# An FNet layer with an MLP in split fp16: x summed into memory in blocks 2 to 5 instead of copied in block 0, and a hand-written order that now reaches over block 1's first step

## The chip, the cores and the metric

The kernel runs on one core of a Trainium2 chip. Its engines, as the profile names them, are TensorE (PE, with its weight loads PEld), VectorE (DVE), ScalarE (ACT), GpSimd (POOL) and SyncE (SP); each runs its instructions in their order, and waits where one needs what another engine or a DMA has not finished. A DMA is issued by an engine (here SP, POOL, and at the start ACT) and then runs by itself on sixteen DMA engines that all queues share. The metric is the device time of one execution in microseconds. The time before is 1279.42 us, the median of three runs from 1277.15 to 1281.52.

## The reference

What is computed, cut to its core (x is 2048 × 576, w1 576 × 4608, w2 4608 × 576, all fp32; w1 and w2 are drawn with a spread of 0.4):

```python
xn = _layernorm(x)                                   # no scale, no shift
a = einsum("bsd,ed->bse", xn, dft_hid_re)
b = einsum("bsd,ed->bse", xn, dft_hid_im)
y = einsum("ts,bse->bte", dft_seq_re, a) - einsum("ts,bse->bte", dft_seq_im, b)
h = maximum(einsum("bsd,df->bsf", xn, w1), 0)
return x + y + einsum("bsf,fd->bsd", h, w2)
```

Every fp32 operand is used as an fp16 high part and an fp16 low part, scaled by a power of two that comes from the operand's largest magnitude; a product is then three matmuls (high by high, high by low, low by high).

## The kernel before

**Tiles and stages.** The 2048 tokens are sixteen tiles of 128 in four groups (g = 0 to 3) of four. The MLP's 4608 hidden columns are nine blocks (b = 0 to 8) of 512. Blocks 1 to 8 are steps (b, g), numbered n = 4 to 35: a step forms the seven products of a Strassen-like scheme for each of two halves (`pair_products`: P1, P2, P6, P5, P7, P3, P4; L498), while the second matmul of the step before it (`products2`, L569) is put between them. What `products2` yields is summed in an SBUF buffer (`blocks2`, L582 and L584), and four buffers a step go by an accumulating DMA of 288 KB on POOL's queue into a DRAM tensor (`add2`, L591, the tiles `spill`). After block 8 the hidden-dimension transform, and then the sequence transform, follow from about 830 us to the end; there x is no longer read, since `spill` holds it already.

**Block 0** does the same in plain products: `piece` and `group` (L396) for the first matmul, 24 matmuls a quarter for the second (`plain2`, L618), ReLU and split (`relu_high`, `relu_low`, L411, L419), a scaled copy (`block2`), and an accumulating DMA (`add0`). In block 0 stands everything that happens once too: loads of x (L149), layernorm statistics (`stats`, L281), the high and low parts of normalised x (L321, L324, L329, L330), and the DMA transposes that make xT of them (`transposes`, L351, on SP; tile 0 alone is transposed on PE, L362). For block 1's scheme sums of xT's quarters are needed: `sums_x`, `high_x`, `low_x` and `transpose_sums` (L470, L473), staged in two buffers.

**What sets the order.** In block 0 the order of all instructions is written by hand, as a table of words, ORDER; each word is a call. The ones that the text uses: `mx` (largest magnitude of a part of w1, L648), `pa` to `pd` (the power of two from it, by PE; L242, L251, then DVE L254 to L259, which gives the scale `c_sw`), `th`, `tl` (PE transposes), `ch_`, `cl` (their copies out of PSUM), `hi`, `xn`, `lo` (high part, centred x, low part), `T` (DMA transposes of a tile), `p0`, `p` (the products of one tile), `P` (those of a group, 512 wide), `m`, `e`, `ad` (second product, its copy, its DMA), `ts`, `tu`, `tv`, `tw` (sums of x: sum, high part, low part, transposes), `lw`, `L1`, `L2` (loads of w2 of block 0, w1 and w2 of block 1), `n*` (block 1's w1), `f` (matmuls on an idle tile, L867, to keep PE busy), and `cx` (x copied from DRAM into `spill`, on SP). Words on different engines go on side by side; on one engine they run in the table's order.

After the table `end_hand()` leaves the order of blocks 1 to 8 to the framework's scheduler, which places instructions by estimated times. There the loads, maxima and splits of the next block's w1 and w2 are a list `todo` of pieces, and the loop over n takes pieces from it at fixed places of a step (`ready`, three a step, and `brief`, seven; in step 4, one more at each call). The transition at the end of block 8 is by hand again.

## Time and profile before

| | |
|---|---|
| median of three runs | 1279.42 us (1277.15 to 1281.52) |
| the profiled execution, time and span | 1281.23 us, span 1279.4 us |
| granted PE clock, mean of the span | 0.992 |
| ACT and POOL busy | 752.7 us (59%), 201.3 us (16%) |
| moved by DMA | 176.30 MB, 138 GB/s on average |
| block 0 | 0 to 118.12 us |

Rows of the profile show the start or the sum in us, the busy time, the engine, the line of the kernel, the operation with its tiles (out<-in), its shape and its count. In a timeline the bracket is the idle time of the engine ahead of the row and what ended it. SPq and PEq are an engine's sequencer. In the table by stretches each engine has its busy time and its count of instructions, then come the granted PE clock (1.00 is full), the mean share in which the 16 DMA engines were busy (rounded from overlapping records, so that it can read above 1) and the bytes they moved.

### The profile page before, as it was taken

How to read it: one execution, taken by the hardware profiler on the slowest of the kernel's cores; microseconds unless marked ns; L12 is line 12 of the kernel's file. 1: busy time of each engine (PE TensorE's matmuls, PEld its weight loads, DVE VectorE, ACT ScalarE, POOL GpSimd, SP SyncE). 2: the span in 40 equal slices, each digit the busy share in tenths (PEclk: the TensorE clock that was granted, in tenths of full speed). 3: DMA queues.
4: the chain of work that ended last, by engine and by line, in shares of the span. 5: the costliest groups of instructions: out<-in, count | busy, mean ns of one | idle time of the engine just before them, and what ended most of it. 6: DMA issues, size and time to landing. Idle time of an engine off the chain costs nothing. (4 is left out here: it accounts for less than half of the span.)

```text
span 1279.4 us, 26178 instructions
## 1 busy us (share of the span) xinstructions
PE 1224.3 (96%) x10403; PEld 996.8 (78%) x10403; DVE 1021.8 (80%) x1974; ACT 752.7 (59%) x1334; POOL 201.3 (16%) x260
## 2 busy tenths in 40 slices
PE   5989899999999999999999999889999999999998
PEld 4956778888888888888887888666777777777777
DVE  7856798888988888788888879769876757888785
ACT  6644767676676676766766757545544445543332
POOL 2353111121111111111111111100111110000000
PEclk9999999999999999999999999989999999999999
DMA  7999756677657566666576677511655541155440
GB/s 214 231 219 215 148 122 142 136 151 153 130 119 160 133 147 134 134 150 124 122 155 140 147 196 165 94 36 67 195 116 148 116 101 24 57 192 160 155 127 33
DMA packets 129387, 176.30 MB, mean 138 GB/s; under 512 B 49648, under 2 KB 90096, under 8 KB 129264
## 3 DMA queue, kind: packets, MB, share of 16 engines
q1 hardware_dynamic: 103344, 127.17, 33.7%
q0 software_dynamic: 25344, 47.20, 26.9%
q8 instruction: 81, 1.33, 0.4%
q14 instruction: 42, 0.34, 0.1%
q10 hardware_dynamic: 576, 0.26, 0.1%
HBM read 112.53 MB, written 56.62 MB: 132 GB/s over the span
## 5 line engine op out<-in xcount | busy, mean ns | idle before, releaser
L569 PE MATMUL p<-w2s,h 128*128 128x288 f16 x2688 | 368.1, 287 | 8.5 <-DVE h L520 2.8
L1349 PE MATMUL p<-R,cs 128*128 128x288 f16 x2688 | 332.6, 287 | 5.6 <-DVE accs L1359 3.3
L1349 PEld LDWEIGHTS <-cs 128*128 128x128 f16 x2688 | 263.2, 98 | 74.9 <-issue 4.5
L569 PEld LDWEIGHTS <-h 128*128 128x128 f16 x2688 | 263.2, 98 | 72.9 <-issue 6.5
L498 PEld LDWEIGHTS <-dbuf 128*128 128x128 f16 x1568 | 153.8, 98 | 31.1 <-issue 9.6
L498 PEld LDWEIGHTS <-wbuf 128*128 128x128 f16 x1568 | 153.4, 98 | 23.8 <-issue 3.0
L766 ACT ACTIVATE cs<-tb,sc_c 128x1024 f16<-128x1024 f32 x56 | 64.0, 1148 | 86.6 <-PE p L1349 53.0
L505 ACT ACTIVATE h<-accs 128x256 f16<-128x256 f32 x128 | 52.2, 412 | 105.3 <-DVE accs L528 82.8
L498 PE MATMUL bank<-xT,dbuf 128*128 128x256 f16 x896 | 112.2, 274 | 0.9 <-ACT s L526 0.9
L498 PE MATMUL bank<-xT,wbuf 128*128 128x256 f16 x896 | 110.7, 273 | 0.0
L591 POOL DMA_DIRECT2D spill<-dbuf x70 | 61.2, 879 | 256.5 <-DVE dbuf L584 215.0
L520 DVE TENSOR_TENSOR h<-s,h 128x1024 f16<-128x1024 f32 x64 | 78.0, 1219 | 28.7 <-ACT h L517 28.4
L498 PE MATMUL bank<-accs,dbuf 128*128 128x256 f16 x672 | 87.1, 273 | 7.1 <-ACT accs L524 5.1
L770 DVE SCALAR_TENSOR_TENSOR cs<-tb,sc_c,cs 128x1024 f16<-128x1024 f32 x56 | 71.6, 1281 | 27.3 <-ACT cs L766 26.9
L498 PE MATMUL bank<-accs,wbuf 128*128 128x256 f16 x672 | 86.4, 272 | 1.9 <-DVE accs L528 1.0
L517 ACT ACTIVATE h<-s 128x1024 f16<-128x1024 f32 x64 | 67.6, 1056 | 20.5 <-DVE s L512 20.1
L766 ACT ACTIVATE cs<-accs,sc_c 128x1024 f16<-128x1024 f32 x39 | 44.2, 1146 | 55.5 <-PE p L1349 25.6
L591 POOL DMA_DIRECT2D spill<-wbuf x42 | 37.1, 884 | 206.2 <-DVE wbuf L584 195.2
L1051 ACT ACTIVATE f<-f 128x1024 f32<-128x1024 f32 x64 | 67.0, 1046 | 0.0
L506 DVE SCALAR_TENSOR_TENSOR h<-accs,h 128x256 f16<-128x256 f32 x128 | 53.0, 418 | 14.0 <-ACT h L505 13.4
L770 DVE SCALAR_TENSOR_TENSOR cs<-accs,sc_c,cs 128x1024 f16<-128x1024 f32 x39 | 50.0, 1281 | 17.1 <-ACT cs L766 16.7
L1169 ACT ACTIVATE R<-tb 128x288 f16<-128x288 f32 (+1 forms) x64 | 39.3, 621 | 38.1 <-DVE tb L1193 29.2
(222 smaller groups left out, 1873.2 us busy)
## 6 DMA issues: line engine op xcount, KB each, us to landing
spill<-dbuf POOLq DMA_DIRECT2D x80, 288.0 KB, 5.1
f<-in_cre_dram SPq DMA_DIRECT2D x32, 512.0 KB, 5.8
f<-in_cim_dram SPq DMA_DIRECT2D x32, 512.0 KB, 4.9
spill<-wbuf POOLq DMA_DIRECT2D x48, 288.0 KB, 4.6
raw_w<-in_w_dram SPq DMA_DIRECT2D x18, 576.0 KB, 5.0
raw_w<-in_w_dram SPq DMA_DIRECT2D x17, 512.0 KB, 5.2
accs<-in_cim_dram SPq DMA_DIRECT2D x16, 512.0 KB, 4.8
tb<-in_cre_dram SPq DMA_DIRECT2D x16, 512.0 KB, 4.6
```

Of the source, the lines that this page charges most:

```text
L498: nc.tensor.matmul(ps, l, r, start=first and m == 0, stop=m == len(todo) - 1, skip_group_check=not first,)
L505: nc.scalar.activation(hi, src, AF.Relu)
L506: stt(lo, src, 0.0, hi, ALU.max, ALU.subtract)
L517: order["s"] = nc.scalar.activation(hi_s, st[:, 1:], AF.Copy).ins
L520: order["lo"] = nc.vector.tensor_tensor(lo_s, st[:, 1:], hi_s, ALU.subtract).ins
L569: nc.tensor.matmul(ps[:, c], h[:, x, qa, c * P : (c + 1) * P], w[:, y, qb], start=first and i == 0 and j == 0, stop=i == NQ - 1 and j == 2 ...
L591: nc.gpsimd.dma_start(spill[g, row, col], sums[row, col], accum_op=ALU.add)
L766: nc.scalar.activation(hi, src, AF.Copy, scale=s)
L770: nc.vector.scalar_tensor_tensor(lo, src, s, hi, ALU.mult, ALU.subtract)
L1051: nc.scalar.activation(f, f, AF.Abs, scale=2.0**-10, accum_out=sums_c[:, n, q : q + 1])
L1169: order["s"] = nc.scalar.activation(hi, src, AF.Copy).ins
L1349: nc.tensor.matmul(ps, w[:, a, RANK[k]], r[:, c, RIGHT[rq]], start=first and k == 0 and j == 0, stop=k == HK - 1 and j == 2, skip_group_ch ...
```

## The change

1. **x into `spill`.** The sixteen words `cx` go, and with them `copy_part`. `add0` writes block 0's sums plainly, where it accumulated before. A new function adds x by sixteen accumulating DMAs on POOL's queue, written into the steps from n = 8 to 23 (blocks 2 to 5), one each.
2. **The table ORDER is new throughout.** It has 120 fills instead of 141. Tile 1 of x, too, is transposed on PE. w2 of block 0 and w1 of block 1 are loaded in another order.
3. **The table goes on into block 1.** `end_hand()` moves behind step n = 4, so the order of this step's instructions is that of the program. Block 1's w2 sums and its power of two (words `rw`, `rm`) are in the table; the power is found on PE.
4. **Loads.** The last rows of w1 are loaded by one pair of DMAs per half, all on SP; before, those of (0, 0) were issued by ACT. `brief` takes no extra piece in step 4. Two kinds of loads for the transforms wait for the last transposes of the sums.

The core of the diff, without the table's rows but for two of each:

```diff
 ORDER = """
-bn:0 ag:0 mx:0 sq:0:0 ch:0:0 bn:1 hi:0 bn:2 xn:0:A th:0 bn:3 ch_:0 lo:0:G ag:2 ag:1 ag:3 mx:1
-sq:2:3 lw:0 sq:1:1 f:27 tl:0 ch:1:1 pa:0 cl:0 pb:0 hi:1 ch:2:3 f:13 pc:0 xn:1:A pd:0 bn:6 wh:0
...
+bn:0 ag:0 mx:0 sq:0:0 ch:0:0 bn:1 hi:0 mx:1 xn:0:A th:0 bn:3 pa:0 ch_:0 lo:0:G pb:0 lw:0 bn:2
+f:10 pc:0 ag:1 ag:3 f:8 tl:0 ag:2 pd:0 sq:1:3 wh:0 ch:1:3 cl:0 wl:0 hi:2 bn:6 f:39 p0:0 xn:2:A
...
+    def load_w1_rest(b, i, r):
+
+        src = w1[b, i].rearrange("p (r k) f -> p r k f", r=2)[:, r, KM]
+        dst = raws["w1", b, i][:, 2 * r : 2 * r + 2, 2]
+        step, size = src.ap[0][0], P - RH
+        both = [[step, size], [RH * step, 2]] + list(src.ap[1:])
+        nc.sync.dma_start(dst[:size], bass.AP(src.tensor, src.offset, both))
+        nc.sync.dma_start(dst[size:], src[: 2 * RH].rearrange("(h p) f -> p h f", h=2))
...
     def add0(g, k):
 
         row, col = BLOCKS0[k]
-        nc.gpsimd.dma_start(spill[g, row, col], sums[row, col], accum_op=ALU.add)
+        nc.gpsimd.dma_start(spill[g, row, col], sums[row, col])
+
+    def add_x(k):
+
+        g, row, col = k // 4, k // 2 % 2, k % 2
+        t = g * TG + row * TG // 2
+        src = x[t * P : (t + TG // 2) * P, :].rearrange("(c p) e -> p c e", p=P)
+        nc.gpsimd.dma_start(spill[g, row, col], src[:, :, col * EH : (col + 1) * EH], accum_op=ALU.add)
...
     def power_w2(b):
 
-        if b:
+        if b > 1:
             yield from power(*(t["w2", b] for t in (sc, pw, mx)))
         else:
...
-            yield from power_pe(sc["w2", b], pw["w2", b], m, *scratch)
+            ps = (banks1[2][1][:, :P], banks1[2][1][:, P:]) if b else scratch
+            yield from power_pe(sc["w2", b], pw["w2", b], m, *ps)
...
+        if b == 1:
+            p = steps1.pop(3)
+            step = lambda: next(p, None)
+            steps = [step, step] + [lambda: None] * 3 + [step, step]
         for i in range(NQ):
             steps += [lambda i=i: split_w2(b, i, 0), lambda i=i: sums_w2(b, i)]
         for i in range(NQ):
-            steps += [lambda: None]
+            steps += [lambda: None] * (b > 1)
             steps += [lambda i=i, c=c: split_w2(b, i, c) for c in (1, 2)]
...
-    load_w1_main(0, 0, slice(0, 1))
-    load_w1_rest(0, 0, nc.scalar)
-    load_w1_main(0, 0, slice(1, 2))
+    for half in range(2):
+        load_w1_main(0, 0, slice(half, half + 1))
+        load_w1_rest(0, 0, half)
...
-    def copy_part(g, c):
-
-        row, col = divmod(c, 2)
-        t = g * TG + row * TG // 2
-        src = x[t * P : (t + TG // 2) * P, :].rearrange("(c p) e -> p c e", p=P)
-        nc.sync.dma_start(spill[g, row, col], src[:, :, col * EH : (col + 1) * EH])
...
+        "rw": lambda i: sum_w2(1, i), "rm": lambda i: steps1.setdefault(3, power_w2(1)).__next__(),
...
-    end_hand()
...
+                with after(order["sp"]):
...
-        nc.sync.dma_start(f, blocks_c(n)[q])
+        with after(order["sp"]):
+            order["sp"] = nc.sync.dma_start(f, blocks_c(n)[q]).ins
...
+        if 2 <= b < 2 + NG:
+            add_x(n - 2 * NG)
...
         ready = lambda q: [work() for _ in range(q + (n == NG))]
-        brief = lambda q: [work(True) for _ in range(q + (n == NG))]
+        brief = lambda q: [work(True) for _ in range(q)]
...
+        if n == NG:
+            end_hand()
```

How it moves instructions, at three places.

**SP, from the transposes of tiles 8 to 11 on.** In the rows xT_136 belongs to group 2 and xT_137 to group 3, accs are x's sums; L351 and L470, L473 before are L345 and L464, L468 in the changed kernel. Before:

```order
L351 DMA_TRANSPOSE xT_136<-dbuf 128x10x128 x4
L907 DMA spill_10_107<-in_x_dram 256x1x288
L470 DMA_TRANSPOSE accs<-wbuf 128x10x128
L907 DMA spill_00_105<-in_x_dram 256x1x288
L907 DMA spill_11_108<-in_x_dram 256x1x288
L907 DMA spill_01_106<-in_x_dram 256x1x288
L470 DMA_TRANSPOSE accs<-wbuf 128x10x128
```

In the changed kernel:

```order
L345 DMA_TRANSPOSE xT_136<-dbuf 128x10x128 x2
L464 DMA_TRANSPOSE accs<-wbuf 128x10x128
L345 DMA_TRANSPOSE xT_136<-dbuf 128x10x128
L464 DMA_TRANSPOSE accs<-wbuf 128x10x128
L345 DMA_TRANSPOSE xT_136<-dbuf 128x10x128
```

The copies between the transposes are gone, and the last of group 2's transposes now has two transposes of sums ahead of it.

**ACT, from the end of block 0 into block 1's first step.** L411 (L405 in the changed kernel) is the ReLU of group 3's last products; L321 and L324 (L315, L318) are high parts of the sums of x; L524 (L521) is the copy that frees the bank of a block 1 product; L629 (L626) is the scaled copy of a sum of block 0. Before, some rows behind the last ReLU:

```order
L629 ACTIVATE wbuf<-p_0_3_0_1803,c_ub 128x576
L321 ACTIVATE wbuf<-accs 128x2x256
L324 ACTIVATE wbuf<-accs 128x2x2x32
L321 ACTIVATE wbuf<-x_99 128x2x256
L324 ACTIVATE wbuf<-x_99 128x2x2x32
L527 ACTIVATE accs<-bank_1782 128x256
L524 ACTIVATE accs<-bank_1779 128x256
```

In the changed kernel, from the last ReLU on:

```order
L405 ACTIVATE h_3_1_1728<-p_0_3_3_1712 128x512
L315 ACTIVATE wbuf<-x_100 128x2x256
L318 ACTIVATE wbuf<-x_100 128x2x2x32
L718 ACTIVATE j_1_1747,c_mw_1651<-raw_w_1_1_1735 128x1152
L521 ACTIVATE accs<-bank_1754 128x256
L626 ACTIVATE wbuf<-p_0_3_0_1778,c_ub 128x576
```

The copy out of the first bank stands ahead of the scaled copy of block 0's sums, with one high part and one maximum of w2 between it and the last ReLU.

**POOL, in block 1, from the last sums of block 0 (L636, in the changed kernel L633) on.** L591 (L588) is `add2`, L640 the new add of x, L208 (L202) the maximum over partitions. Before:

```order
L636 DMA spill_11_116<-wbuf 128x576
L591 DMA spill_00_101<-wbuf 128x576
L208 ISA top<-c_mw_2134 128x1
L591 DMA spill_11_104<-dbuf 128x576
L591 DMA spill_01_102<-dbuf 128x576
L591 DMA spill_10_103<-wbuf 128x576
L591 DMA spill_00_105<-dbuf 128x576
```

In the changed kernel:

```order
L633 DMA spill_11_116<-wbuf 128x576
L588 DMA spill_00_101<-wbuf 128x576
L640 DMA spill_00_101<-in_x_dram 256x1x288
L588 DMA spill_11_104<-dbuf 128x576
L588 DMA spill_01_102<-dbuf 128x576
L588 DMA spill_10_103<-wbuf 128x576
L202 ISA
L202 ISA top<-c_mw_2267 128x1
L640 DMA spill_01_102<-in_x_dram 256x1x288
L588 DMA spill_00_105<-dbuf 128x576
```

An x add follows the sum that goes into the same block, and the next sums stand behind it. The scheduler puts the sixteen adds on POOL between the sums of steps 5 to 20, most of them ahead of their step in the program.

## The prediction

> **What bounds the kernel now.** I began with the page's table of engines, then took the list of PE's waits, then busy time by stretches, and the timelines last.

> ```profile
> span 1279.4 us, 26178 instructions
> PE 1224.3 (96%) x10403; PEld 996.8 (78%) x10403; DVE 1021.8 (80%) x1974; ACT 752.7 (59%) x1334; POOL 201.3 (16%) x260
> ```

> PE works in 1224.3 of 1279.4 us, so only 55.1 us can be won without removing matmuls. Their places:

> ```profile
> PE p L362 <- ACT dbuf L321: 12.0, 1, 12.0
> PE p L396 <- DMA xT<-dbuf: 6.2, 3, 3.3
> PE bank L498 <- ACT accs L524: 5.6, 4, 4.0
> ```

> The columns are the sum, the count and the longest, in us. The first is the start; the second is block 0's product of xT waiting for its transposes; the third is the first steps of block 1. All three lie in what the table ORDER or its end touches.

> ```profile
> core 0: us, PE busy (x) PEld busy (x) DVE busy (x) ACT busy (x) POOL busy (x), PEclk, DMA share, GB/s
> 30.00:60.00 30.00, 28.12 (x426) 26.37 (x426) 25.27 (x68) 21.34 (x39) 11.21 (x14) 1.00 1.09 247
> 60.00:90.00 30.00, 26.66 (x164) 16.14 (x162) 17.01 (x37) 14.01 (x26) 17.04 (x22) 0.94 1.18 208
> 90.00:120.00 30.00, 30.00 (x201) 19.29 (x200) 23.79 (x48) 15.34 (x27) 11.52 (x13) 1.00 1.14 242
> 160.00:400.00 240.00, 237.07 (x2047) 199.95 (x2046) 206.43 (x459) 167.97 (x327) 42.99 (x53) 1.00 0.67 142
> ```

> From 30 to 120 us the 16 DMA engines have no free time (share 1.09 to 1.18); in blocks 1 to 4 a third is free (0.67). From 160 to 400 PE loses 2.9 us of 240. So the change can win in the first 150 us and only lose afterwards.

> ```profile
> 12.03 0.61 PE L362 MATMUL p<-ident,dbuf 128*128 128x128 f16 x4 [12.03 <-ACT dbuf L321]
> 17.94 3.90 PE L867 MATMUL p<-dbuf 128*128 128x128 f16 x67 [0.25 <-DVE half L254]
> 21.67 0.94 PE L396 MATMUL p<-xT,wbuf 128*128 128x128 f16 x14
> 27.61 1.72 PE L396 MATMUL p<-xT,wbuf 128*128 128x128 f16 x28 [0.90 <-DMA xT<-dbuf]
> 31.88 7.98 PE L396 MATMUL p<-xT,wbuf 128*128 128x128 f16 x140 [1.93 <-DMA xT<-dbuf]
> 70.86 10.91 PE L396 MATMUL p<-xT,wbuf 128*128 128x512 f16 x42 [3.34 <-DMA xT<-dbuf]
> 106.03 12.25 PE L396 MATMUL p<-xT,wbuf 128*128 128x512 f16 x56
> 118.12 1.69 PE L498 MATMUL bank<-xT,dbuf 128*128 128x256 f16 x14
> 129.36 1.26 PE L498 MATMUL bank<-accs,dbuf 128*128 128x256 f16 x7 [3.98 <-ACT accs L524]
> ```

> This is PE's timeline; the bracket is the idle time ahead. Block 0 ends at 118.12.

> **The start.** Everything there hangs on the first maximum of w1.

> ```profile
> 9.14 0.95 DVE L648 TENSOR_REDUCE c_mf<-raw_w 128x1 f32<-128x768 f32 x1 [4.12 <-DMA accs<-in_x_dram]
> 11.16 0.81 ACT L321 ACTIVATE dbuf<-accs,sh,r 128x512 f16<-128x512 f32 x1 [5.82 <-DVE sh L302]
> 17.92 0.15 DVE L255 TENSOR_SCALAR c_sw<-half 128x1 int32<-128x1 int32 x1
> 20.37 1.38 SPq L351 DMA_TRANSPOSE xT<-dbuf  x1
> 26.59 1.42 SPq L351 DMA_TRANSPOSE xT<-dbuf  x1
> ```

> DVE idles 4.12 us until 9.14 for the four small loads of w1's last rows, which ACT's queue issues. The change puts half 0's two on SP right behind its main load: by SP's issue times of 0.6 us they leave by 3.1, so I estimate the maximum at 7 to 8 and th:0 near 10.9 instead of 12.03. x tiles 1 to 3 then leave some 2.5 us later; bn:1 waits for one of them, still far less than 4 us. The second half's maximum follows straight behind, so the scale (c_sw, 17.92) comes near 13.5 to 14, and p0:0 near 17.5 (was 21.67).

> Behind p0:0 the order has 63 fills of 58 ns (3.90/67), 3.65 us, some ten transposes and the second power, so p0:1 starts near 23.2. Against a stream without gaps: before, 84 pieces stand ahead of the 140 at 31.88, 57 ns each, so its start was 31.88 − 4.8 = 27.1. Afterwards it is 23.2 − 0.8 (p0:0's 14 pieces) = 22.4, plus the new waits. Tile 2's transpose came to use 5.3 us after its issue (26.59 to 31.88). Tile 5's must be in use at 36.4 by PE's sum; its remainder, by DVE's and POOL's durations in the new order, ends near 33.1, so it lands at 37.5 to 38.4 or, with tile 2 late too, 39: a wait of 1.1 to 2.6, up to 0.7 more for tile 2. Gain 27.1 − 22.4 − (1.1 to 3.3) = 1.4 to 3.6 us; I take **1.8**, near the low end, since the row nearest to it is a wait of this kind (1.93). The 21 fills removed and 10 transposes added are inside these times.

> **The transposes of group 1.** The 3.34 us at 70.86 is the wait for tiles 4 to 7's and 8 to 11's transposes behind a full DMA.

> ```profile
> 54.06 12.60 SPq L351 DMA_TRANSPOSE xT<-dbuf  x4
> spill<-in_x_dram SPq DMA_DIRECT2D x16, 288.0 KB, 5.7
> 72.00:74.00 2.00, 2.00 (x6) 0.73 (x5) 0.00 (x0) 0.00 (x0) 0.00 (x0) 0.50 1.20 294
> 130.00:132.00 2.00, 2.00 (x10) 1.31 (x9) 0.43 (x1) 1.75 (x4) 0.00 (x0) 0.50 0.63 118
> 32.00:34.00 2.00, 2.00 (x39) 2.00 (x38) 0.77 (x2) 0.78 (x3) 0.82 (x1) 1.00 1.05 383
> ```

> SP held four transposes for 12.60 us. The 16 copies leave (a column of the DMA list: 5.7 us to landing, 4.6 MB, sixteen issues of 0.6 us), so does the read half of block 0's sums in DRAM. After the change P:2 would be reached near 68.6 and its last transpose issues near 57 and lands by 62: 6 us of margin. The stall goes, and with it a slow clock: the third row shows 0.50 of full clock after 3.34 us idle, the fourth the same after 3.98, the fifth full clock after 1.93. At half clock some 3.4 us of matmuls do 1.7 us of work. Worth 3.34 + 1.7 = **5.0**; if the new order makes a wait of its own here, 0.

> [...]

> **Block 1's first step.** PE waits 3.98 us because ACT does:

> ```profile
> 127.94 0.63 ACT L321 ACTIVATE wbuf<-x 128x512 f16<-128x512 f32 x1 [3.01 <-DMA xT<-wbuf]
> 128.94 0.65 ACT L524 ACTIVATE accs<-bank 128x256 f32<-128x256 f32 x2
> ```

> A high part for group 3's sums waits 3.01 us for its staging buffer, and the copies that free the product's bank stand behind it. The scheduler set this. In hand order, two of these parts are still ahead of the first bank copy; they wait for a transpose that goes out about when block 0 ends, so the copy comes 3.6 to 4.6 us into the step, where the product that needs the bank comes at 4.5: a stall of 0 to 2. Removed: 3.98 + 1.6 (clock, computed as above). Gain 3.6 to 5.6; I take **4.3**. Step 2's waits were 2.4 us in sum; block 1's w2 splits come just in time there now (1 to 3 us), so nothing.

> **The x sums in blocks 2 to 5.** Sixteen more accumulating DMAs on POOL, which the scheduler spreads over steps 5 to 20, some 350 us.

> ```profile
> 189.31 0.88 POOL L591 DMA_DIRECT2D spill<-wbuf  x1 [8.85 <-DVE wbuf L584]
> q0 software_dynamic: 6459, 13.23, 40.2%
> spill<-dbuf POOLq DMA_DIRECT2D x28, 288.0 KB, 4.9
> POOL top L208 <- DVE c_mw L657: 13.9, 5, 3.7
> ```

> From 160 to 400 the 44 such DMAs take 40.2% of the engines: 0.402 × 240 / 44 = 2.2 us each, so 16 add 35 us over 350, lifting 0.67 to 0.77. No saturation. Each must wait for the sum into the same block before it (landing 4.9), and on POOL it holds the next sums and the maxima (L208), for which the scales wait. POOL's gap before a step's first sum is 8.85 us, and in twelve of sixteen places the add falls into it; elsewhere a sum leaves 2 to 3 us late, against buffers with about 3.5 us of slack. I take **0**; below nothing there is no reason, and the upper end is 4 adds × 1.5 us = 6 us.

> [...]

> **Preparation later.** Step 1 pops six pieces of preparation fewer from the list. A step pops ten in about 21 us, so w1 and w2 of blocks 2 to 8 become ready 13 us later.

> ```profile
> 388.42 1.53 DVE L770 SCALAR_TENSOR_TENSOR w2s<-raw_w,c_sw,w2s 128x576 f16<-128x576 f32 x2
> 406.23 1.63 PE L569 MATMUL p<-w2s,h 128*128 128x288 f16 x12
> PE p L569 <- DVE h L520: 2.8, 3, 1.3
> ```

> Block 4's last w2 splits end at 389.95, 16 us before the first product that uses block 4's w2 (406.23), 22 before the third. 13 of them go. In the new order the last split stands three DVE instructions ahead of the second product's evacuation, with an estimated 3.5 to 5 us left of DVE's lag. So the term is 0, at the other end some 2.2 us at each of 7 block ends.

> The loads for the transform that stood between SP's transposes (two at 21.8 to 26.5) now go out behind them; their use is after 820 us: 0 to +1, I take 0.5.

> **Sum.** 1.8 + 5.0 + 4.3 = 11.1, less 0.5, less 2.2 for waits that an order this new makes where I have not looked (one of the size of the 1.93 row): **8.4 us**. From the profiled span of 1279.4 (its run took 1281.23; the median shown is 1279.42) this gives **1271.0**.

> **Rivals.** *One stall stays or is replaced* (a T wait that hi and lo parts, not the DMA, set; removing copies then does not do what it is for): for it speaks the 5.3 us of one transpose before the heavy DMA even began; against it the share of 1.18. Gain 4 to 5: 1275. *POOL holds up the maxima*: 6 us lost, 1277; for it the 3.7 us wait of L208, against it the 8.85 us gap. *All gains, no new waits*: 11 to 14 with the start at 3.6 and no T:5 wait: 1266. *Slower, the late w2 splits*: PE stands at each of 7 block ends for DVE, whose order is fixed. It decides once DVE's lag at a step's end passes 5 us. At 2.2 us each this is 15.4 on −11.1 with the discount gone: 1283.7. For it: DVE at 206.43 of 240 us, 86%, and PE's longest wait for h, 1.3 us; against it: that wait comes only three times in the run.

> **Chances.** Likeliest (its own range 1267 to 1275) 0.42; one stall 0.14; POOL 0.12; all gains 0.13; late splits 0.19. A measurement of this kernel tells 0.3%, 3.8 us, from none. Faster: 0.42 + 0.13 and half of one stall and of POOL, 0.68; slower: three quarters of the last, 0.14; same: the rest, 0.18. The range, 1263 to 1284, runs from beyond full gains to the late splits.

> **What would show it.** Right: PE's first product at 17 to 18; no wait above 2.6 us on xT and block 0's end near 111; no 3 us wait of ACT on the staging buffer, nor of PE on its copy; PE's idle from 160 to 800 near that of before. Wrong: waits of PE for w2s at 7 places of equal distance, POOL waits before L208 above 5 us, or a clock of 0.50 anywhere in the first 150 us. Most of all the forecast falls if the new order has a T wait over 3 us.

## The result, and the profile after

| kernel | median | ratio to the kernel before, 95% interval |
|---|---|---|
| before | 1279.54 us (20 runs, 1275.22 to 1283.56) | 1 |
| changed | 1281.61 us (20 runs, 1278.25 to 1285.16) | 1.0018 [1.0008, 1.0028] |

The change did not gain 8.4 us; it cost 2.1 (1.0 to 3.6 by the interval). The two profiled executions happen to have the same span:

```profile
span 1279.4 us, 26160 instructions
PE 1222.7 (96%) x10394; PEld 993.2 (78%) x10394; DVE 1019.5 (80%) x1968; ACT 754.3 (59%) x1334; POOL 213.9 (17%) x279
```

PE's timeline of the changed kernel in block 0 and block 1's first step (start, busy time, row, and in brackets the idle time ahead):

```profile
8.26 0.61 PE L356 MATMUL p<-ident,dbuf 128*128 128x128 f16 x4 [8.26 <-ACT dbuf L315]
16.00 0.94 PE L390 MATMUL p<-xT,wbuf 128*128 128x128 f16 x14
22.48 1.72 PE L390 MATMUL p<-xT,wbuf 128*128 128x128 f16 x28 [0.17 <-DMA xT<-dbuf]
65.83 12.25 PE L390 MATMUL p<-xT,wbuf 128*128 128x512 f16 x56 [0.34 <-DMA xT<-dbuf]
89.29 6.04 PE L615 MATMUL p<-w2s,h 128*128 128x288 f16 x48 [1.93 <-ACT dbuf L626]
110.66 1.69 PE L495 MATMUL bank<-xT,dbuf 128*128 128x256 f16 x14
116.86 0.92 PE L495 MATMUL bank<-accs,dbuf 128*128 128x256 f16 x7 [1.56 <-ACT accs L521]
```

Block 0 ends at 110.66 where it ended at 118.12; the wait of 3.34 us for xT is one of 0.34, that of 3.98 for the bank is 1.56. The forecast gain of the first 150 us is there. It is given back later. In the list of PE's waits the row for transposes (6.2 us before) has 0.7, and the row of a DVE sum which frees a bank, small before, now leads. Before:

```profile
PE bank L498 <- DVE accs L528: 2.6, 3, 1.0
```

In the changed kernel:

```profile
PE bank L495 <- DVE accs L525: 8.7, 9, 2.0
PE p L356 <- ACT dbuf L315: 8.3, 1, 8.3
PE bank L495 <- ACT accs L521: 3.8, 4, 1.6
PE p L390 <- DMA xT<-dbuf: 0.7, 3, 0.3
```

By stretches, PE's idle time from 160 to 400 us is 240 − 230.49 = 9.5 us; before it was 2.9:

```profile
core 0: us, PE busy (x) PEld busy (x) DVE busy (x) ACT busy (x) POOL busy (x), PEclk, DMA share, GB/s
60.00:90.00 30.00, 27.73 (x181) 17.35 (x180) 20.39 (x44) 17.21 (x35) 15.07 (x23) 1.00 0.99 184
160.00:400.00 240.00, 230.49 (x1976) 192.89 (x1974) 194.83 (x436) 160.38 (x311) 52.50 (x63) 1.00 0.71 145
```

Where the lead goes is seen step by step. The mark is the start of ACT's scaled copy of a step's first second-layer product (L582 before, L579 in the changed kernel; in the two kernels on the right L580), and the table has its time minus that of the kernel before, in us. Two profiles of the changed kernel differ by 0.5 to 2.0 us in it. 36 stands for the transition behind the last step; the kernels on the right are the experiments below.

| step | before, at | changed | without the adds | same places | last three moved |
|---|---|---|---|---|---|
| 5 | 151.84 | −11.5 | −10.9 | −12.0 | −10.1 |
| 9 | 240.10 | −11.5 | −10.5 | −11.9 | −9.8 |
| 10 | 261.46 | −8.3 | −9.9 | −11.0 | −8.8 |
| 16 | 386.92 | −5.1 | −6.7 | −7.8 | −5.6 |
| 17 | 409.04 | −0.8 | −6.3 | −7.4 | −5.2 |
| 21 | 494.42 | −1.5 | −7.0 | −8.5 | −5.9 |
| 22 | 515.97 | −0.1 | −8.6 | −4.0 | −7.5 |
| 35 | 797.15 | −4.3 | −12.9 | −8.0 | −11.2 |
| 36 | 816.20 | −1.1 | −11.5 | −5.3 | −8.5 |

The changed kernel falls behind the one without adds at three places: 2.6 us between steps 9 and 10, 4.0 between 16 and 17, 2.9 between 21 and 22. That makes 9.5 us; elsewhere up to step 35 the distance between the two moves by no more than 1 us. The second of these places, engine by engine (POOL, POOL, DVE, ACT, PE):

```profile
387.55 1.04 POOL L640 DMA_DIRECT2D spill<-in_x_dram  x1 [6.04 <-DMA spill<-wbuf]
388.15 0.79 POOL L202 PARTITION_ALL_REDUCE top<-c_mw  x1
388.98 0.17 DVE L205 TENSOR_SCALAR half<-top 128x2 f32<-128x2 f32 x1 [3.96 <-POOL top L202]
390.31 1.01 ACT L771 ACTIVATE w2s<-raw_w,c_sw 128x864 f16<-128x864 f32 x1 [5.04 <-DVE c_sw L742]
390.66 0.92 PE L495 MATMUL bank<-accs,wbuf 128*128 128x256 f16 x7 [2.04 <-DVE accs L525]
```

An add of x waits 6.04 us on POOL for a sum to land. The maximum of w2 stands behind it; DVE, in its fixed order, waits 3.96 us for that; the sum that frees PE's bank (L525) stands behind DVE's wait; PE waits 2.04. ACT waits 5.04 for the scale by the same way. At the first place it is the maximum of w1, with one add ahead of it:

```profile
247.07 1.05 POOL L640 DMA_DIRECT2D spill<-in_x_dram  x1 [2.29 <-DMA spill<-dbuf]
248.50 0.15 DVE L205 TENSOR_SCALAR half<-top 128x1 f32<-128x1 f32 x1 [3.18 <-POOL top L202]
251.10 1.69 PE L495 MATMUL bank<-accs,wbuf 128*128 128x256 f16 x14 [1.57 <-ACT accs L521]
```

### The profile page after: what moved, and what is told of

The parts are those of the page before. It is cut to its first block, busy times and chain, and to the rows that moved or that the text cites. A ratio compares the mean times of both kernels' runs of the same rounds, so it can differ in the third digit from the quotient of the medians.

```text
span 1279.4 us, 26160 instructions
## 1 busy us (share of the span) xinstructions
PE 1222.7 (96%) x10394; PEld 993.2 (78%) x10394; DVE 1019.5 (80%) x1968; ACT 754.3 (59%) x1334; POOL 213.9 (17%) x279
## 4 chain that ended last, share of the span: by engine, by line
PE 53%; DVE 19%; issue 12%; DMA 6%; ACT 5%; POOL 3%; SPq 1%; POOLq 0%; DVEq 0%; ACTq 0%
PE p L1358 20%; PE p L566 13%; PE bank L495 13%; PE pd L1211 6%; DMA raw_w<-in_w_dram 2%; POOL spill L588 2%; DVE h L517 1%; DVE cs L775 1%; DVE h L503 1%; DVE R L1171 1%; DVE w2s L775 1%; DMA accs<-in_x_dram 1%; DMA accs<-in_cim_dram 1%; DMA raw_d<-in_dft_dram 1%; ACT f L1056 1%
## 5 line engine op out<-in xcount | busy, mean ns | idle before, releaser
L566 PEld LDWEIGHTS <-h 128*128 128x128 f16 x2688 | 262.2, 98 | 74.7 <-issue 10.1
L495 PEld LDWEIGHTS <-wbuf 128*128 128x128 f16 x1568 | 153.3, 98 | 31.5 <-issue 10.5
L588 POOL DMA_DIRECT2D spill<-dbuf x70 | 63.3, 923 | 190.7 <-DVE dbuf L581 165.4
L775 DVE SCALAR_TENSOR_TENSOR cs<-tb,sc_c,cs 128x1024 f16<-128x1024 f32 x56 | 71.5, 1281 | 27.5 <-ACT cs L771 27.1
L588 POOL DMA_DIRECT2D spill<-wbuf x42 | 38.2, 910 | 190.7 <-DVE wbuf L581 172.7
## 6 DMA issues: line engine op xcount, KB each, us to landing
spill<-dbuf POOLq DMA_DIRECT2D x80, 288.0 KB, 4.7
spill<-wbuf POOLq DMA_DIRECT2D x48, 288.0 KB, 5.0
```

Of the source, the lines that this page charges most:

```text
L495: nc.tensor.matmul(ps, l, r, start=first and m == 0, stop=m == len(todo) - 1, skip_group_check=not first,)
L566: nc.tensor.matmul(ps[:, c], h[:, x, qa, c * P : (c + 1) * P], w[:, y, qb], start=first and i == 0 and j == 0, stop=i == NQ - 1 and j == 2 ...
L588: nc.gpsimd.dma_start(spill[g, row, col], sums[row, col], accum_op=ALU.add)
L775: nc.vector.scalar_tensor_tensor(lo, src, s, hi, ALU.mult, ALU.subtract)
```

## The experiments

All were timed against the kernel before on the same chip, in five rounds; ratios are to that kernel. 0.1% is 1.3 us.

**1. Without the adds of x.**

```diff
-        if 2 <= b < 2 + NG:
-            add_x(n - 2 * NG)
```

> The changed kernel without its sixteen adds of x (the output lacks x). The trace of the changed kernel is 11.4 us ahead of the one before at the start of block 1's second step, and loses this lead between 240 and 520 us. POOL theory: the adds wait for the landing of a sum on POOL and hold the maxima over partitions behind them, for which DVE and then PE wait; without the adds the lead stays: 8 to 11 us less than the changed kernel, 1271 to 1274. Preparation theory: the lead is lost because w1 and w2 of the next blocks come 13 us later; then the time stays at 1280 to 1282.

Measured: 1272.73 us, ratio 0.9920 [0.9898, 0.9943]. Against the changed kernel's 1.0018 the adds cost 0.98%, 12.5 us (the two intervals together leave 9 to 16). The three places make 9.5 of it, and the two profiled spans, 1279.4 and 1270.6, differ by 8.8; where the rest goes, if there is more, is not shown. Without the adds the kernel is as fast as the forecast, or a little faster. At the place of the second loss DVE's row has no wait:

```profile
383.48 0.17 DVE L205 TENSOR_SCALAR half<-top 128x2 f32<-128x2 f32 x1
```

**2. Preparation earlier again.**

```diff
-        brief = lambda q: [work(True) for _ in range(q)]
+        brief = lambda q: [work(True) for _ in range(q + (n == NG))]
```

> The changed kernel with the six extra pieces of preparation taken in step 4 again. Preparation theory: w1 and w2 are ready 13 us earlier and the lead stays: 1272 to 1276. POOL theory: the maxima are asked for earlier but are held as before; no more than 1.5 us of difference, 1280 to 1283.

Measured: ratio 1.0028 [1.0007, 1.0049]. Not the cause.

**3. The kernel before with the x adds.** One part of the change alone: the sixteen words `cx` go, and

```diff
-        nc.gpsimd.dma_start(spill[g, row, col], sums[row, col], accum_op=ALU.add)
+        nc.gpsimd.dma_start(spill[g, row, col], sums[row, col])
...
+        if 2 <= b < 2 + NG:
+            add_x(n - 2 * NG)
```

> The kernel before with one part of the change alone: the words cx are taken out of its table, block 0's sums are written plainly, and x is added in steps 8 to 23 as in the changed kernel. If the copies caused the 3.34 us wait for xT in block 0, that wait and its slow clock go (5 us less). POOL theory: then 8 to 11 us are lost to the adds: 1282 to 1286 in all. Preparation theory: nothing is lost to them: 1274 to 1276.

Measured: 1289.74 us, ratio 1.0056 [1.0039, 1.0073]; on that chip the kernel before had 1282.84. The wait for xT is gone, PE going on without a gap and at full rate (9.23 us for 42 matmuls that took 10.91):

```profile
54.75 11.92 PE L618 MATMUL p<-w2s,h 128*128 128x288 f16 x96
66.51 9.23 PE L396 MATMUL p<-xT,wbuf 128*128 128x512 f16 x42
```

**4. The kernel before without copies and without adds.** As 3, without its last two lines.

> The kernel before without its sixteen copies of x and with plain writes of block 0's sums, x left out altogether. By the forecast's step on group 1's transposes, the copies' traffic causes the 3.34 us wait at 70.86 and its slow clock: 5 us less, ratio 0.996 and no such wait in the trace. Rival: the transposes are late for their own reasons; then the wait stays and the ratio is 1.000.

Measured: 1275.52 us, ratio 0.9963 [0.9950, 0.9976]; of the 3.34 us wait 0.60 is left. So the copies cost 4.7 us, and by run 3 the adds 0.93%, 11.9 us, in the old order too: where the scheduler puts the adds, moving x into blocks 2 to 5 is a loss by itself, with the old table ORDER as with the new.

**5. The adds spread**, one a step, aimed at another token group.

```diff
-            add_x(n - 2 * NG)
+            with after(order["acc"]):
+                add_x((n + 1) % NG * 4 + (n - 2 * NG) // NG)
```

> The changed kernel with the same sixteen adds, one in each step, placed behind the previous step's last DVE sum and aimed at another token group, so that fewer stand right behind the sum into their own block or right ahead of a maximum. POOL theory: most of the loss comes back, 1273 to 1277. If it is the adds' traffic and not their waits that costs, the time stays at 1280 to 1282, as by the preparation theory.

Measured: 1276.39 us, ratio 0.9953 [0.9935, 0.9972]. Two thirds of the loss come back, but not for the reason expected. The adds now stand one to about every four sums, and all sixteen still wait on POOL for a sum to land, 55.9 us in all:

```profile
POOL spill L640 <- DMA spill<-dbuf: 31.9, 10, 5.4
POOL spill L640 <- DMA spill<-wbuf: 24.0, 6, 6.7
```

In the changed kernel fourteen wait, 52.2 us in all. So POOL's waiting as such is not what costs. Between 140 and 520 us DVE's longest wait for a maximum is 1.9 us here and 4.0 in the changed kernel.

**6. The adds without a wait, in tiles of their own**, at the places that run 9 lists.

```diff
-        nc.gpsimd.dma_start(spill[g, row, col], src[:, :, col * EH : (col + 1) * EH], accum_op=ALU.add)
+        nc.gpsimd.dma_start(park[k], src[:, :, col * EH : (col + 1) * EH], accum_op=ALU.add)
...
+            for k in range(NT):
+                with after(order["sp"]):
+                    nc.sync.dma_start(park[k], x[:P, :].rearrange("p (r e) -> p r e", r=2))
```

> The changed kernel with its sixteen adds of x at the same places of POOL's queue and of the same size, but into sixteen DRAM tiles of their own, which sixteen plain copies on SP fill in block 1; so no add waits for the landing of a sum (the output lacks x). POOL theory, with the wait as the cause: as without the adds, 8 to 11 us less than the changed kernel. Traffic theory (the adds' own load on the DMA engines and on POOL): no more than 2 us less than the changed kernel.

Measured: ratio 1.0037 [1.0021, 1.0052], a miss of this run's own making. Its sixteen copies stand on SP ahead of a load for block 2, and PE stops before the first add comes:

```profile
174.76 3.14 PE L497 MATMUL bank<-accs,dbuf 128*128 128x256 f16 x14 [8.55 <-ACT accs L523]
```

It tells nothing of the waits; run 9 asks the same without the copies.

**7. The adds behind a step's first sum.**

```diff
+            i = nc.gpsimd.dma_start(spill[g, row, col], sums[row, col], accum_op=ALU.add)
+            if n == 1:
+                order["first"] = i.ins
...
+        def m(q):
+            mlp2(pb, pg, q)
+            if q == 1 and 2 <= b < 2 + NG:
+                with after(order["first"]):
+                    add_x((n + 1) % NG * 4 + (n - 2 * NG) // NG)
```

> The changed kernel with one add of x a step, queued on POOL right behind the step's first sum and aimed at the token group whose sums landed two steps before, so that it finds nothing to wait for. POOL theory: as without the adds but for their issue, 16 x 1 us that lies in POOL's gaps of 8 us: ratio to the kernel before 0.992 to 0.995. Traffic theory: no better than the adds that were spread, or 1.000.

Measured: 1273.95 us, ratio 0.9949 [0.9929, 0.9968]: 8.8 us less than the changed kernel by the ratios, and 6.5 less than the kernel before, with the whole computation done. None of its adds waits. Its ratio is no better than run 5's 0.9953 by more than the noise, so a gain from waiting for nothing, beyond that of spreading, is not shown by the times.

**8. As 7, with the hidden transform's loads free** (`with nullcontext():` for `with after(order["sp"]):` in `load_dk`).

> The kernel with the adds behind the first sum, and the loads of the hidden transform's matrix no longer queued behind the last transposes and the loads of the sequence transform. If these loads come late at 800 to 840 us, 1 to 3 us less than the kernel that it is made from; if they have slack, no difference beyond 1 us.

Measured: ratio 0.9983 [0.9969, 0.9997], 4.4 us more than 7. No gain late, and about half of the loss early: the table's mark at step 5 is 8.8 us ahead of the kernel before, where run 7 has 10.8. That the loads stand in block 0 again fits this, but between kernels with the same block 0 this mark spreads from 10.1 to 13.0, so the place of the loss is not shown.

**9. The same places, no waits.** The adds stand on POOL where the changed kernel has them, but their targets are turned by two token groups.

```diff
+            i = nc.gpsimd.dma_start(spill[g, row, col], sums[row, col], accum_op=ALU.add)
+            order["count"] = order.get("count", 0) + 1
+            for k, at in enumerate((1, 4, 19, 20, 21, 24, 24, 38, 41, 43, 44, 44, 45, 63, 64, 64)):
+                if at == order["count"]:
+                    with after(i.ins):
+                        add_x((k + 2 * NG) % NT)
```

> The changed kernel with the sixteen adds of x at the same places of POOL's queue, each into a tile of spill, but the targets turned by two token groups, so that each add's last sum landed about two steps before and nothing is waited for. This has the changed kernel's traffic, bytes and places and lacks only the waits. Theory of the waits: as without the adds or with the adds behind the first sum, ratio 0.992 to 0.996. Theory of traffic or of the places: 1.001 to 1.003 as the changed kernel.

Measured: ratio 1.0000 [0.9984, 1.0016], beside both expectations. The table of marks says why. Up to step 21 the lead is that of the kernel without adds (−8.5 and −7.0): both losses by waits are gone. Then 4.5 us go at once. DVE's wait there, PE's, and the loads of w1 (a row of the DMA list from 480 to 515 us: count, KB each, median us to landing):

```profile
DVE c_mf L658 <- DMA raw_w<-in_w_dram: 6.3, 1, 6.3
498.90 1.57 PE L496 MATMUL bank<-accs,dbuf 128*128 128x256 f16 x7 [2.89 <-DVE s L527]
raw_w<-in_w_dram SPq DMA_DIRECT2D x4, 96.0 KB, 13.9
```

In the kernel without adds these loads land in 6.7 us, in the changed kernel in 10.3, and there DVE waits 3.2:

```profile
raw_w<-in_w_dram SPq DMA_DIRECT2D x4, 96.0 KB, 6.7
```

```profile
raw_w<-in_w_dram SPq DMA_DIRECT2D x4, 96.0 KB, 10.3
```

```profile
DVE c_mf L652 <- DMA raw_w<-in_w_dram: 3.2, 1, 3.2
```

In run 9 three adds go out together at 480 to 483 us, ahead of the loads. In the changed kernel two of them go out at 488.5 and 490.9, among the loads (488.6 to 500.5), and the third waits until 498.3. This is the changed kernel's third loss: DVE waits for a load and not for POOL, and what delays the load is the traffic of a bunch. Without their waits the three are closer together, and it is larger. Run 10 tests this.

**10. The last three adds moved.** As 9, with places 49, 53 and 57 for 63, 64 and 64.

> The kernel with the adds at the same places and turned targets, but the last three, which go out bunched at 480 to 483 us right ahead of the loads of w1 for a later block, are put behind the first sums of steps 17, 18 and 19. In the trace of the kernel with the same places that is where it loses its lead, 4.5 us between steps 21 and 22, while DVE waits 6.3 us for w1. Theory of two causes (the waits cost 6 to 7 us in two places, the bunch's traffic 3 to 5 us in a third): that wait goes, ratio 0.993 to 0.997. If the loss came from elsewhere: 0.999 to 1.002.

**11. The changed kernel beside it.**

> The changed kernel itself on the same chip, for comparison with the run beside it: 1.001 to 1.003, 3 to 10 us above it by the theory of two causes.

Measured: run 10 has 1274.34 us, ratio 0.9952 [0.9935, 0.9968], the changed kernel 1.0009 [0.9991, 1.0027]. In run 10 the loads land in 7.2 us, DVE waits for none of them, and between steps 21 and 22 nothing is lost (−5.9 to −7.5). The changed kernel loses at the same three places as in its first profile (2.6, 4.0 and 4.3 us against the marks of the kernel without the adds).

**12. Step 1 ordered by the scheduler.** The kernel of run 1, with `end_hand()` behind the table.

> The changed kernel without its adds of x (the output lacks x), with the order by hand ending before step 4 as in the kernel before, so that the scheduler orders block 1's first step. By the forecast's step on block 1 the hand order there is worth 3.6 to 5.6 us: then the time is that much above the same kernel without the adds. Rival: the table's own rows removed that wait, since the last high parts stand earlier in it; then the difference is below 1.5 us.

Measured: ratio 0.9943 [0.9923, 0.9963] against run 1's 0.9920 [0.9898, 0.9943]. The difference is 2.9 us, between the two expectations, and with an interval of about −1 to 7 us the times exclude neither. The traces say more. At mark 36 this kernel is 11.8 us ahead of the kernel before, run 1's 11.5; the 2.4 us by which its span is longer (1273.0, 1270.6) arise behind that mark, for a reason that is not shown. In block 1's first step its longest wait is 1.07 us, with the hand order 1.46.

```profile
118.39 0.22 PE L236 MATMUL bank<-ident,mb 128*2 128x128 bf16 x1 [1.07 <-DVE mb L728]
```

```profile
117.41 0.92 PE L495 MATMUL bank<-accs,dbuf 128*128 128x256 f16 x7 [1.46 <-ACT accs L521]
```

So the wait of 3.98 us went with the table's own rows, whoever orders step 1, and not with the copies: runs 3 and 4, with the old table and without copies, still have 3.29 and 3.34 us there. That it went because the last high parts come earlier in the table fits, but is not tested alone.

## Why the prediction was wrong, point by point

- **What failed: the x sums in blocks 2 to 5.** I took 0 and an upper end of 6 us; they cost 12.5 by the ratios, of which 9.5 are found in the traces: 6.6 by two maxima behind a waiting add, 2.9 by a bunch. I set POOL's gaps of 8.85 us against a landing of 4.9 and called the adds hidden, with late sums as the price ("4 adds × 1.5 us"). It is not a mean gap that counts but what stands behind each wait: in run 5 the adds wait as long (55.9 us, 52.2 in the changed kernel), and two thirds of the loss are gone. The count of twelve adds in a long gap holds, but w2's maximum lies in such a gap too. The add ahead of it came after the step's last sum, waited 6.04 us, and two engines waited for the maximum. The prediction named that chain as a rival ("POOL holds up the maxima", 0.12) and priced it at 6 us; the two places together are 6.6. The order of POOL was known for this: adds with a maximum next to them could have been counted and each followed to DVE.
- **What was missing: bunches.** I raised the share of the DMA engines from 0.67 to 0.77 on the average and saw no saturation. The measured average is 0.71, and still three adds close together made a load of w1 land in 10.3 us instead of 6.7, with DVE in order behind it: 2.9 us.
- **The start**: right in sign, too small. I estimated the first maximum at 7 to 8 us and PE's first transpose at 10.9; the trace has 5.37 and 8.26, and p0:0 at 16.00 (17.5). The waits of 1.1 to 3.3 us for tiles 2 and 5 were 0.17 and nothing. From the start of group 2's products back: 70.86 − 65.83, plus 3.05 for the 24 matmuls now ahead of it, less the 3.34 of the wait, is 4.7 us, where I took 1.8 with 3.6 as the end. Not all of it need be the table's: in run 4, with the old table and no copies, these products come 2.0 us earlier, their wait left out, 0.9 of it from a first transpose at 11.11 instead of 12.03.
- **The transposes of group 1**: right, but for the name: the four transposes at 54.06 and the products at 70.86 are group 2's. 5.0 forecast; 4.7 us by run 4, the wait 0.34 us and the clock 1.00 from 60 to 90 us. Fewer fills brought no loss of clock in this trace: no idle time of PE between 8.26 and 400 us is longer than 2.04, and the clock is 1.00 from 0 to 400 us. In run 7, with the same table, 48 matmuls of block 0 took 7.71 us where run 9 has 6.04; the last section comes to that.
- **Block 1's first step**: forecast 4.3. PE's lead grows from 7.5 us at the step's start to 9.4 at step 5's first product (147.91 before, 138.54 now), and to 11.5 by the mark. The size is nearly right by the marks, the cause half wrong (run 12). From 120 to 150 us the clock is 1.00, where it was 0.94 before. That a wait of this length costs the 1.6 us was not sure either: ACT copies a later product of this step out of its bank 6.63 us after the copy that PE waited for in run 3, behind a wait of 3.29 us (122.21, 128.84), 7.80 in run 4, behind 3.34 (121.91, 129.71), and 7.94 in the kernel before, behind 3.98 (128.94, 136.88).
- **Preparation later**: 0 was right (run 2), and the slower rival built on it fell: there are no waits for w2s at seven places.
- **The transform's loads**: I charged 0.5 for ordering them late; run 8 has 4.4 us the other way.
- **Discount of 2.2**: block 0 has one new wait of this size, 1.93 us for a sum's buffer.

Without the adds the kernel gains 0.8% (10.2 us; the forecast was 8.4). That the two are so close is partly luck, since the start was worth some 3 us more than I took. The term that turned the sign is the adds alone. Of the signs named, block 0's end near 111 came, and of those for a wrong forecast the wait of POOL above 5 us ahead of a maximum. The range up to 1284 holds the result, but for the sake of the late w2 splits, which did not come.

The adds of x did not overlap the sums into their own blocks: in the changed kernel POOL stands with an add in ten waits for a sum to land between 160 and 400 us, 38.7 us in all. Run 9, with the targets turned, has none there.

```profile
POOL spill L640 <- DMA spill<-dbuf: 19.8, 6, 4.6
POOL spill L640 <- DMA spill<-wbuf: 18.9, 4, 6.4
```

## What to carry to other kernels

A DMA with something to wait for costs what is queued behind it on its engine, instruction by instruction (here 6.04 us on POOL, 3.96 on DVE and 2.04 on PE): look for the one small operation (here a maximum over partitions) that another engine waits for in order. An average share of the DMA engines (here 0.71) says little of a bunch ahead of a load that is due (landed in 10.3 us instead of 6.7). If work is moved off a full stretch, choose its targets so that it finds nothing to wait for, and give each piece its own gap: by the ratios the same sixteen adds cost 12.5 us as the scheduler placed them, and some 4 us, hardly clear of noise, where they are one a step (runs 5 and 7). The kernel of run 7 (1273.95 us, ratio 0.9949) beats both the kernel before and the changed one. Of the two pieces of advice, the ratios bear out the gap of its own; finding nothing to wait for is shown to help only at the two places where a maximum stood behind the wait (run 9).

## What the runs showed of the hardware that was not expected

```profile
498.00:500.00 2.00, 1.10 (x6) 0.81 (x6) 2.00 (x5) 1.12 (x3) 0.00 (x0) 0.75 0.99 243
500.00:502.00 2.00, 2.00 (x11) 1.23 (x9) 2.00 (x8) 0.33 (x2) 0.35 (x1) 0.50 0.47 149
502.00:504.00 2.00, 2.00 (x17) 1.59 (x16) 1.66 (x3) 1.20 (x2) 0.88 (x1) 0.89 0.01 2
```

The length of the gap does not decide alone. Behind an idle time of 2.16 us the same 48 matmuls of block 0 take 7.71 us in run 7 (first row) and 6.04 in run 9 (second):

```profile
89.80 7.71 PE L617 MATMUL p<-w2s,h 128*128 128x288 f16 x48 [2.16 <-ACT dbuf L628]
90.32 6.04 PE L621 MATMUL p<-w2s,h 128*128 128x288 f16 x48 [2.16 <-ACT dbuf L632]
```

The 1.67 us between them are what some 3.4 us at half clock would cost, by my estimate from run 9's rows. They are part of the spread of the marks at step 5. Run 6 has such a pair in one trace: behind 1.97 us 56 matmuls take 13.93 us, where the changed kernel has 12.25 and no loss of clock, and behind 2.02 us 7 matmuls take 0.93, as at full clock:

```profile
68.27 13.93 PE L392 MATMUL p<-xT,wbuf 128*128 128x512 f16 x56 [1.97 <-DMA xT<-dbuf]
119.35 0.93 PE L497 MATMUL bank<-accs,dbuf 128*128 128x256 f16 x7 [2.02 <-ACT accs L523]
```

So a wait of about 2 us cost some 1.7 us more in these traces, or nothing; what decides it, besides the length, is not shown.
